# One attention-and-MLP kernel: reads put ahead of feature maps, first loads cut in pieces, and the weights' low bits moved to another engine

## The chip, the cores and the metric

The kernel runs on one core of one Trainium2 chip. The metric is the device time of one execution in microseconds, as the median of several runs; smaller is better. The engines are TensorE (PE, matmuls; PEld its weight loads), VectorE (DVE), ScalarE (ACT), GpSimd (POOL) and SyncE (SP), whose queue issues most DMAs.

## The reference

```python
scores = scale * q @ k.T                       # 4 batches, 8 heads, 576 tokens, 64 wide, causal
a = exp(scores - max); a /= a.sum() + 1e-9
local = a @ v
q_p = phi(q)                                   # where(x > 0, x, exp(x) - 1) + 1
mem_out = (q_p @ M_prev) / (q_p @ z_prev + 1e-6)
g = 1 / (1 + exp(-beta))
x = (g * mem_out + (1 - g) * local)            # reshaped to 2304 tokens x 512
out = (silu(x @ w_gate) * (x @ w_val)) @ w_out # 1536 hidden columns
```

q, k, v and the memory are float32; the three weight matrices are float64.

## The kernel before

Every fp32 operand of a large matmul is split into a high and a low part, and a product is three matmuls (high with high, high with low, low with high). The program has two stages.

**Attention.** The 32 head matrices are taken as 16 pairs. The loop at L532 runs 17 periods: period n does the scores and the softmax of pair n (`cur`) and, for pair n - 1 (`old`), the turning of the probabilities by transposes on TensorE (`turned`, `turned1`), the recall from the memory (`recall`), the products with v (`recalled`, `values`) and the result (`leave`, then `ending` in the next period, which casts the high part on ScalarE, subtracts the low part on VectorE and writes both to DRAM). Scores of one pair come in five steps t into the four banks `s`; VectorE reads a bank, adds the mask and finds the row's maximum (`reading`, the instruction CUSTOM_DVE_ANT_0), ScalarE takes the exponential (`exp`), VectorE inverts the sums (`rs`), and GpSimd scales the probabilities with the inverse and the gate (`weighed`, tiles `ps`, `pl` and `p`). The transposes and the products use four banks `tr` in turn. The work of each engine is kept in program order by `queued` (L79), so the order of the calls in the loop is the order on that engine. SP's DMAs and a few instructions that are issued by the bare engine names, such as `ACT.copy` at L279, are placed by the scheduler.

The first period is written out apart: `pair_load` (L248) loads q and k of a pair whole, for pair 0 with k from ScalarE's queue; `pair_split` cuts pair 0 in two column pieces; `phi_parts` (L326) makes the feature map of q with two ScalarE steps and one VectorE step (`SCALAR_TENSOR_TENSOR ph`); `gates` (L141) makes g and 1 - g from beta in two VectorE parts, `one_less` (needed by the first `weighed`) and `memory` (needed by the recall). In the first period `memory_gates`, `phi0` and the map of pair 1 come behind the exponential of step 4 (L594 to L597).

**Experts.** The hidden columns are 12 units f of 128, and the 2304 tokens are three blocks of 768 (L30). The first three units of the first block (`PLAIN`) compute gate and value straight (`eight`, four products of 12 matmuls); all others use a scheme with seven half-size products (`seven`) whose operands are sums and differences of weight quarters (`operands`) and of token quarters (`sums`). Two banks take the products in turn, six collect the output. A product's bank is free again when ScalarE has copied it or VectorE has weighed it (`weigh`).

Each unit has three weight matrices (gate, value, output): 36 "thirds" of 128 x 512 float64 words, made into fp32 in the first block and kept in DRAM for the other two. A third goes through: `raw_load` (DMA from SP), `raw_top` (ScalarE brings the upper word to scale, tile `we`, two buffers), `third_clamp` (tile `we`), `third_move` (the three bits of the lower word, tile `wa` or `wr`), `third_word` (VectorE joins both, SP writes it out, ScalarE casts the high part where it is wanted at once) and `low_part` (VectorE). The clamp and the move of the first four thirds run on VectorE within the attention (`EARLY`, L31), all others on GpSimd within the units of the first block (`third`, L234, at the steps of `plan`). On GpSimd the move reads only the last byte of the lower word, as

```python
eng.tensor_scalar(wa[n], last_byte, 1.0 / 32, 31.0 / 64, op0=ALU.mult, op1=ALU.subtract)
```

`plan[k]` lists what is issued behind product k of a unit. The sums of the first block's tokens (`due`) and their high and low parts (`spreads`, for p6, p5, p3, p7) are dealt out by hand over the first units at L880 to L893.

Of the kernel before, what the change touches and what calls it, by code (L numbers as in the profile page):

```python
# [9 lines left out]
F32 = mybir.dt.float32  # L10
F32R = mybir.dt.float32r
I32 = mybir.dt.int32
U8 = mybir.dt.uint8
AF = mybir.ActivationFunctionType
# [7 lines left out]
NP = B * NPAIR  # L22
# [22 lines left out]
def attention_moe(ctx: ExitStack, tc: tile.TileContext, qt, kt_, v, m, beta, wg, wv, wo, out):  # L45
# [70 lines left out]
    DVE.memset(warm, 0.0)  # L116
    ACT.activation(warm, warm, AF.Exp)
    maskp = const.tile([128, 512], F32, name="maskp")
    POOL.memset(maskp, 0.0)
# [42 lines left out]
    held, wout, wr = {}, {}, {}  # L162
    thirds = [(0, 0), (0, 1), (0, 2), (1, 0)]
    work_of = [[(1, 1), (3, 0), (3, 1)]]
    work_of += [[(n, 2)] + [(n + 1 + (n >= PLAIN - 1), j) for j in range(2)] for n in range(1, NF - 2)]
# [17 lines left out]
    def raw_top(act, n):  # L183
        if n < len(thirds):
            tops[n] = rot(wp, "we", [128, 512], F32, 2)
            act.activation(tops[n], raws[n][:, :, 1].bitcast(F32), AF.Prelu, scale=2.0**-111, alpha=2.0**32)
# [13 lines left out]
    def third_move(eng, n):  # L200
        f, j = thirds[n]
        if f < PLAIN or j == 2:
            wa[n] = rot(wp, "wa", [128, 512], I32, 3)
        else:
            if j == 0:
                wr[f] = rot(wp, "wr", [128, 1024], F32, 2)
            wa[n] = wr[f][:, j * 512 : j * 512 + 512].bitcast(I32)
        if eng is dve:
            eng.tensor_scalar(wa[n], raws[n][:, :, 0], 29, None, op0=ALU.logical_shift_right)
        else:  # L210
            last_byte = raws[n].rearrange("p a b -> p (a b)").bitcast(U8).rearrange("p (a b) -> p a b", b=8)[:, :, 3]
            eng.tensor_scalar(wa[n], last_byte, 1.0 / 32, 31.0 / 64, op0=ALU.mult, op1=ALU.subtract)

# [30 lines left out]
    with tc.tile_pool(name="sb", bufs=1, reuse_waits="tile") as sb:  # L244
# [3 lines left out]
        def pair_load(n):  # L248
            b, pr = divmod(n, NPAIR)
            qr = rot(sb, "qr", [128, 768], F32, NR)  # L250
            kr = rot(sb, "kr", [128, 576], F32, NR)
            for dst, src in ((qr, qt), (kr, kt_)):
                queue = ACT if n == 0 and dst is kr else SP
                loads[n] = queue.dma_start(dst, src[b, pr])
            return qr, kr
# [276 lines left out]
        for n in range(NP + 1):  # L532
# [6 lines left out]
            if cur:  # L539
                cur.begin()  # L540
            if old:
                old.turns()
# [7 lines left out]
            reads[1](0)  # L550
            reads[1](1)
            if after and n:
                after.split()
# [5 lines left out]
            turned(2, 0, dve)  # L559
            turned(2, 1, dve)  # L560
            exp(1, 1)
            scale = old.recall() if old else nothing
# [31 lines left out]
            if n == 0:  # L594
                memory_gates()
                phi0()
                phi = after.phi_parts()  # L597
            if old:
                old.recalled()
                old.values()  # L600
            if cur:
                cur.weighed(((2, 0), (2, 1), (3, 0), (3, 1)))
            phi()
            if cur:
                cur.weighed(((4, 0),))
            ending = old.leave() if old else lambda: nothing
# [5 lines left out]
            for i, at in enumerate(EARLY):  # L612
                if n == at:
                    raw_top(act, i)
                if n == at + 1:
                    third_clamp(dve, i)
                if n == at + (2 if i < 3 else 1):
                    third_move(dve, i)
                if n == at + (3 if i < 3 else 2):
                    third_word(act, dve, i)  # L620
                if n == at + (4 if i < 3 else 2):
                    low_part(dve)
            if n in AHEAD:
                raw_load(AHEAD.index(n), loads.get(n + 2))

        n = len(EARLY)
        raw_load(n + 3)
        raw_top(act, n)
        raw_top(act, n + 1)
        third_clamp(pool, n)  # L630
        third_move(pool, n)
        ending()()

    nj = N2 // 128
    with tc.tile_pool(name="stg2", bufs=1, reuse_waits="tile") as stg2, \
# [220 lines left out]
        for n, unit in enumerate(units):  # L856
# [14 lines left out]
            if n < len(units) - 1 and n + 1 >= PLAIN:  # L871
                ready[n + 1], work = operands(units[n + 1][1])
                if plain:
                    work = [work[0] + work[1], work[2], work[3], work[4] + work[5] + work[6]]
                for k, some_ in enumerate(work):
                    plan[k] += some_
# [3 lines left out]
            if plain:  # L880
                if f == 0:
                    _, due, mix = sums(t0, True)
                if f < 2:
                    for k in range(4):
                        plan[k].append(due[4 * f + k])
                if f == 1:
                    plan[2] += spreads(mix, ("h", "p6"))
                    plan[3] += spreads(mix, ("l", "p6"))
                if f == PLAIN - 1:
                    for k, p in ((0, "p5"), (1, "p3")):  # L890
                        plan[k] += spreads(mix, ("h", p))
                        plan[k + 2] += spreads(mix, ("l", p))
                    arrive = [(0, spreads(mix, ("h", "p7"))), (1, spreads(mix, ("l", "p7")))]  # L893
# [91 lines left out]
```

## Time and profile before

| | us |
|---|---|
| median of 3 runs | 626.1 (625.47 to 626.37) |
| the profiled execution | 626.68 |
| its span | 624.9 |
| TensorE busy in it | 604.7 |
| attention, to the first expert matmul | 193.9 |
| first token block, with the weights' conversion | 193.9 to about 345 |

All helper instructions carry one line (L84), so groups are told apart by tile names: `pl<-pl,rs,og` is a scaling, `s<-kh,qh` a matmul of scores, `wr<-wraw` a move of low bits. In a timeline a row has the start, the duration, the engine, the tiles, the shape and, in brackets, the idle time of that engine before it and the releaser. A busy TensorE is not TensorE at its best: its clock is in a column of its own.

### The profile page before, as it was taken

To read this page: it belongs to the slowest core of one execution; us is meant where nothing else is said; L and a number is where in the kernel's file an instruction comes from. 1 tells how busy PE (TensorE), PEld (TensorE's weight loads), DVE (VectorE), ACT (ScalarE), POOL (GpSimd) and SP (SyncE) were. 2 spreads that over 40 slices of the span, in tenths; PEclk is the share of its full clock that TensorE was granted. 3 is DMA by queue.
4 is the path that set the end of the run, shared out by engine and by line. 5 is a ranking of instruction groups with operands and counts; after the bars stand their busy time and mean duration, and the time that the engine had idled before them with its cause. 6 is when DMAs were issued, how large, how long until landed. Compare 5 with 4: busy or idle time off the path is not lost.

```text
span 624.9 us, 11274 instructions
## 1 busy us (share of the span) xinstructions
PE 604.7 (97%) x3794; PEld 534.9 (86%) x3794; DVE 494.7 (79%) x1209; ACT 383.5 (61%) x892; POOL 268.1 (43%) x282
## 2 busy tenths in 40 slices
PE   5999999999999899999999999999999999999997
PEld 3777788778778798988889999999999999999995
DVE  6799899999986899999999666566788765665653
ACT  6788888888875467666657644455446654454442
POOL 6899999999965986867740000000000000000000
PEclk9799999999999999999999999999999999999999
DMA  8355856757435775799638532232756631332212
GB/s 244 96 157 172 268 163 188 239 161 212 150 100 172 217 238 183 237 294 314 218 135 286 168 117 88 72 128 71 238 172 214 202 102 67 102 102 67 70 33 101
DMA packets 48745, 102.46 MB, mean 164 GB/s; under 512 B 6960, under 2 KB 16176, under 8 KB 48688
## 3 DMA queue, kind: packets, MB, share of 16 engines
q1 hardware_dynamic: 48544, 101.45, 50.1%
q8 instruction: 30, 0.49, 0.3%
q10 hardware_dynamic: 144, 0.29, 0.1%
q14 instruction: 27, 0.22, 0.1%
HBM read 74.99 MB, written 26.74 MB: 163 GB/s over the span
## 4 chain that ended last, share of the span: by engine, by line
PE 80%; DVE 9%; POOL 4%; ACT 3%; issue 2%; DMA 1%; DVEq 0%; POOLq 0%
PE s L84 50%; PE tr L84 30%; ACT pl L84 2%; DVE xr L84 1%; POOL we L84 1%; POOL wa L84 1%; DVE tl L84 1%; POOL wr L84 1%; DVE rs L84 1%; DVE pl L84 1%; DVE mem L84 1%; DMA kr<-in_kt_dram 1%; DVE zh L84 1%; ACT g L84 1%; DVE wa L84 1%
## 5 line engine op out<-in xcount | busy, mean ns | idle before, releaser
L84 POOL TENSOR_SCALAR pl<-pl,rs,og 128x384 f32<-128x384 f32 (+1 forms) x64 | 56.0, 886 | 10.9 <-DVE rs L84 10.9
L84 ACT ACTIVATE zh<-zh 128x384 f32<-128x384 f32 x33 | 17.3, 526 | 70.4 <-DVE zh L84 70.3
L84 PE MATMUL tr<-woh,uh 128*128 128x512 f32 x144 | 57.3, 398 | 0.0
L84 PE MATMUL tr<-wol,uh 128*128 128x512 f32 x144 | 56.7, 394 | 0.0
L84 PE MATMUL tr<-woh,ul 128*128 128x512 f32 x144 | 56.6, 393 | 0.0
L84 DVE TENSOR_TENSOR zv<-s,zv 128x384 f32<-128x384 f32 x33 | 18.3, 556 | 47.7 <-PE s L84 47.5
L84 ACT CAST th<-tt 128x512 fp32r<-128x512 f32 x66 | 41.0, 622 | 18.2 <-DVE tt L84 14.9
L84 ACT ACTIVATE pl<-pl,mx 128x384 f32<-128x384 f32 (+1 forms) x64 | 42.3, 663 | 14.2 <-DVE mx L84 14.2
L84 PE MATMUL tr<-g,vp 128*64 128x320 f32 (+4 forms) x448 | 48.7, 360 | 0.0
L84 DVE TENSOR_TENSOR tl<-tt,th 128x512 fp32r<-128x512 f32 x66 | 46.9, 711 | 0.0
L84 PE MATMUL s<-kh,qh 64*128 64x128 f32 (+4 forms) x160 | 37.6, 389 | 7.4 <-ACT kh L84 5.4
L84 PEld LDWEIGHTS tr<-g,vp 128*64 128x64 f32 x448 | 29.5, 137 | 17.6 <-issue 2.3
L84 POOL TENSOR_SCALAR we<-we 128x512 f32<-128x512 f32 x32 | 30.1, 940 | 28.1 <-ACT we L84 25.8
L84 POOL TENSOR_SCALAR wr<-wraw 128x512 int32<-128x512 uint8 x18 | 38.5, 2136 | 1.4
L84 DVE TENSOR_TENSOR zg<-s,zp 128x384 f32<-128x384 f32 x33 | 18.4, 558 | 25.9 <-ACT bh L84 20.6
L84 DVE CUSTOM_DVE_ANT_0 pl<-s,maskp 128x384 f32<-128x384 f32 (+1 forms) x64 | 38.1, 615 | 0.7 <-PE s L84 0.7
L84 ACT CAST uh<-zh 128x384 fp32r<-128x384 f32 x36 | 18.5, 514 | 29.7 <-DVE zh L84 29.4
L84 DVE TENSOR_TENSOR bl<-wr,bh 128x512 fp32r<-128x512 f32 x66 | 36.5, 553 | 0.0
L84 PE MATMUL tr<-ident,pl 128*128 128x128 f32 x224 | 32.3, 281 | 2.3 <-DVE xl L84 1.6
L84 POOL TENSOR_SCALAR ps<-ps,rs,og 128x128 f32<-128x128 f32 (+1 forms) x64 | 31.9, 511 | 6.0 <-DVE rs L84 5.1
L84 ACT CAST bh<-wr 128x512 fp32r<-128x512 f32 x66 | 33.9, 513 | 0.0
L84 DVE COPY g<-tr 128x384 f32<-128x384 f32 (+1 forms) x64 | 32.0, 519 | 2.1 <-PE tr L84 0.8
(187 smaller groups left out, 2031.6 us busy)
## 6 DMA issues: line engine op xcount, KB each, us to landing
wr<-wdr SPq DMA_DIRECT2D x24, 512.0 KB, 3.3
qr<-in_qt_dram SPq DMA_DIRECT2D x16, 384.0 KB, 3.1
wraw<-in_wg_dram SPq DMA_DIRECT2D x12, 512.0 KB, 4.4
wraw<-in_wv_dram SPq DMA_DIRECT2D x12, 512.0 KB, 4.8
wraw<-in_wo_dram SPq DMA_DIRECT2D x12, 512.0 KB, 4.4
wol<-wdo SPq DMA_DIRECT2D x24, 256.0 KB, 2.8
woh<-wdo SPq DMA_DIRECT2D x24, 256.0 KB, 3.2
vp<-in_v_dram SPq DMA_DIRECT2D x16, 320.0 KB, 4.4
```

The lines of the kernel that those rows point to most:

```text
L84: ins = getattr(eng, name)(*args, **kw)
```

## The change

Six things are edited.

1. Pair 0's q and k are loaded in five column pieces, three from SP and two from ScalarE's queue, those wanted first ahead.
2. The last scaling of pair 0, its feature map and the memory's gates (`late`) are issued in period 1 behind that period's first four reads; the VectorE step of pair 1's map goes to the end of period 1.
3. `third_move` for gate and value thirds runs on ScalarE (an Identity activation with scale and bias) where it ran on GpSimd; a bias tile is set at the start.
4. Third (1, 1) joins the early ones: in the last period its top, clamp, move and word are done, and so are the word of third (1, 0), which was already there, and the top of the next. The raw loads of thirds 7 and 8 follow. `we` has three buffers.
5. Silu's table is loaded at the start of the last period by an activation of one column.
6. In the plain units the sums, the spreads of p5 and the operands of unit 3 are dealt out over other steps.

```diff
+    low_bias = const.tile([128, 1], F32, name="low_bias")
+    DVE.memset(low_bias, -31.0 / 64)
...
-    thirds = [(0, 0), (0, 1), (0, 2), (1, 0)]
-    work_of = [[(1, 1), (3, 0), (3, 1)]]
+    thirds = [(0, 0), (0, 1), (0, 2), (1, 0), (1, 1)]
+    work_of = [[(3, 0), (3, 1)]]
...
-            tops[n] = rot(wp, "we", [128, 512], F32, 2)
+            tops[n] = rot(wp, "we", [128, 512], F32, 3)
...
             eng.tensor_scalar(wa[n], raws[n][:, :, 0], 29, None, op0=ALU.logical_shift_right)
+            return
+        last_byte = raws[n].rearrange("p a b -> p (a b)").bitcast(U8).rearrange("p (a b) -> p a b", b=8)[:, :, 3]
+        if j == 2:
+            eng.tensor_scalar(wa[n], last_byte, 1.0 / 32, 31.0 / 64, op0=ALU.mult, op1=ALU.subtract)
         else:
...
+            act.activation(wa[n], last_byte, AF.Identity, scale=1.0 / 32, bias=low_bias)
...
-            for dst, src in ((qr, qt), (kr, kt_)):
-                queue = ACT if n == 0 and dst is kr else SP
-                loads[n] = queue.dma_start(dst, src[b, pr])
+            if n == 0:
+                for queue, dst, src, c in (
+                    (SP, qr, qt, slice(128, 384)), (ACT, kr, kt_, slice(0, 256)), (SP, qr, qt, slice(384, 768)),
+                    (ACT, kr, kt_, slice(256, 576)), (SP, qr, qt, slice(0, 128)),
+                ):
+                    queue.dma_start(dst[:, c], src[b, pr, :, c])
+            else:
+                for dst, src in ((qr, qt), (kr, kt_)):
+                    loads[n] = SP.dma_start(dst, src[b, pr])
...
+            if n == NP:
+                act.activation(warm, warm, AF.Silu)
             if old:
                 old.turns()
...
             reads[1](1)
+            if n == 1:
+                for work in late:
+                    work()
             if after and n:
                 after.split()
...
             turned(2, 1, dve)
+            if n == NP:
+                for i in range(2):
+                    raw_top(act, len(EARLY) + i)
+                third_clamp(pool, len(EARLY))
+                third_move(pool, len(EARLY))
...
             if n == 0:
-                memory_gates()
-                phi0()
-                phi = after.phi_parts()
+                phi1 = after.phi_parts()
+            if n == NP:
+                for i in range(2):
+                    third_word(act, dve, len(EARLY) - 1 + i)
+                    raw_load(len(EARLY) + 3 + i)
...
-            phi()
-            if cur:
-                cur.weighed(((4, 0),))
+            if n == 0:
+                late = [lambda cur=cur: cur.weighed(((4, 0),)), phi0, memory_gates]
+            else:
+                if n == 1:
+                    phi1()
+                phi()
+                if cur:
+                    cur.weighed(((4, 0),))
...
-                if n == at + (3 if i < 3 else 2):
+                if n == at + 3 and i < 3:
                     third_word(act, dve, i)
-                if n == at + (4 if i < 3 else 2):
+                if n == at + 4 and i < 3:
                     low_part(dve)
...
-        n = len(EARLY)
-        raw_load(n + 3)
-        raw_top(act, n)
-        raw_top(act, n + 1)
-        third_clamp(pool, n)
-        third_move(pool, n)
         ending()()
+        low_part(dve)
+        i = len(EARLY) + 1
+        third_clamp(pool, i)
+        third_move(pool, i)
+        raw_top(act, i + 1)
...
-                    work = [work[0] + work[1], work[2], work[3], work[4] + work[5] + work[6]]
+                    work = [work[0] + work[1], work[2] + work[3], work[4] + work[5], work[6]]
...
-                if f < 2:
-                    for k in range(4):
-                        plan[k].append(due[4 * f + k])
+                    for k, some_ in enumerate(((0,), (1,), (2, 4), (3,))):
+                        plan[k] += [due[i] for i in some_]
                 if f == 1:
-                    plan[2] += spreads(mix, ("h", "p6"))
-                    plan[3] += spreads(mix, ("l", "p6"))
+                    for k in range(3):
+                        plan[k].append(due[5 + k])
+                    for k, p in ((0, "p5"), (2, "p6")):
+                        plan[k] += spreads(mix, ("h", p))
+                        plan[k + 1] += spreads(mix, ("l", p))
                 if f == PLAIN - 1:
-                    for k, p in ((0, "p5"), (1, "p3")):
-                        plan[k] += spreads(mix, ("h", p))
-                        plan[k + 2] += spreads(mix, ("l", p))
+                    plan[0] += spreads(mix, ("h", "p3"))
+                    plan[2] += spreads(mix, ("l", "p3"))
```

## Rows read from the trace of the kernel before

**Rows 1.** The page, part 1: busy us, share of the span, instructions.

```profile
PE 604.7 (97%) x3794; PEld 534.9 (86%) x3794; DVE 494.7 (79%) x1209; ACT 383.5 (61%) x892; POOL 268.1 (43%) x282
```

**Rows 2.** Timeline of PE, the first two periods, rows after idle time.

```profile
5.38 0.47 PE L84 MATMUL s<-kh,qh 64*128 64x128 f32 x2 [5.38 <-ACT kh L84]
...
13.82 0.38 PE L84 MATMUL s<-kh,qh 64*128 64x256 f32 x2 [1.39 <-DVE mx L84]
...
15.59 0.69 PE L84 MATMUL tr<-ident,ps 128*128 128x128 f32 x2 [0.56 <-POOL ps L84]
...
17.50 0.90 PE L84 MATMUL tr<-ident,pl 128*128 128x128 f32 x3 [0.30 <-POOL pl L84]
```

**Rows 3.** Windows: length, busy us by engine, granted clock, DMA share, GB/s.

```profile
15.50:22.00 6.50, 6.09 (x26) 4.75 (x28) 4.31 (x19) 4.40 (x13) 5.72 (x9) 0.50 0.19 61
22.00:24.00 2.00, 2.00 (x19) 1.59 (x16) 1.48 (x7) 1.07 (x3) 2.00 (x5) 0.99 0.06 12
```

**Rows 4.** Timeline of PE, the first token block, rows after idle time.

```profile
202.97 0.45 PE L84 MATMUL s<-xp1h,wgh 128*128 128x384 f32 x1 [0.47 <-ACT zh L84]
...
207.47 0.44 PE L84 MATMUL s<-xp1h,wgh 128*128 128x384 f32 x1 [2.11 <-DVE zh L84]
...
236.34 0.44 PE L84 MATMUL s<-xp7l,th 128*128 128x384 f32 x1 [0.56 <-DVE xp7l L84]
```

**Rows 5.** Waits of PE, whole span: us in total, times, longest.

```profile
PE s L84 <- DVE zg L84: 1.5, 4, 0.4
```

**Rows 6.** Timelines of ACT and POOL at the start: casts that wait for loads.

```profile
4.83 0.76 ACT L84 CAST kh<-kr 128x256 fp32r<-128x256 f32 x2 [2.18 <-DMA kr<-in_kt_dram]
...
8.37 0.67 ACT L279 CAST kh<-kr 128x576 fp32r<-128x576 f32 x1 [1.51 <-DMA kr<-in_kt_dram]
...
7.58 0.84 POOL L84 TENSOR_SCALAR qh<-qr 128x640 fp32r<-128x640 f32 x1 [1.89 <-DMA qr<-in_qt_dram]
```

**Rows 7.** The page, part 6: a DMA of 256 KB, median us to landing.

```profile
wol<-wdo SPq DMA_DIRECT2D x24, 256.0 KB, 2.8
```

**Rows 8.** Timelines of DVE and POOL, 14 to 17.5 us: feature maps and scalings.

```profile
14.30 0.81 DVE L84 SCALAR_TENSOR_TENSOR ph<-qe,ph 128x640 f32<-128x640 f32 x1
...
15.96 0.95 DVE L84 SCALAR_TENSOR_TENSOR ph<-qe,ph 128x640 f32<-128x640 f32 x1 [0.56 <-ACT ph L84]
...
14.33 1.21 POOL L84 TENSOR_SCALAR ps<-ps,rs,og 128x256 f32<-128x256 f32 x1
...
16.22 1.22 POOL L84 TENSOR_SCALAR pl<-pl,rs,og 128x384 f32<-128x384 f32 x1
```

**Rows 9.** Groups of POOL by shape, 184.1 to 187.3 us: busy, mean ns.

```profile
L84 POOL TENSOR_SCALAR pl<-pl,rs,og 128x384 f32<-128x384 f32 x2 | 1.3, 661 | 3.5 <-DVE rs L84 3.5
```

**Rows 10.** Timelines of ACT, DVE and PE in the last period and behind it.

```profile
195.41 1.28 ACT L84 ACT_TABLE_LOAD   x1
...
185.10 0.43 ACT L84 CAST xh<-tr 128x320 fp32r<-128x320 f32 x1 [0.45 <-PE tr L84]
...
185.99 0.48 DVE L84 TENSOR_TENSOR xl<-tr,xh 128x320 fp32r<-128x320 f32 x1
...
186.62 0.52 PE L84 MATMUL tr<-ident,pl 128*128 128x128 f32 x3 [0.43 <-POOL pl L84]
```

**Rows 11.** Groups of POOL, and of ACT from 190 us: busy, mean ns, idle before.

```profile
L84 POOL TENSOR_SCALAR wr<-wraw 128x512 int32<-128x512 uint8 x18 | 38.5, 2136 | 1.4
...
L84 ACT ACTIVATE we<-wraw 128x512 f32<-128x512 f32 x32 | 21.4, 672 | 8.8 <-DVE wr L84 8.6
```

**Rows 12.** Windows, one unit of the first block; busy PE, PEld, DVE, ACT, POOL.

```profile
255.00:266.50 11.50, 11.50 (x61) 10.70 (x61) 10.26 (x19) 7.31 (x16) 9.21 (x7) 1.00 0.70 229
```

**Rows 13.** Timeline of DVE ahead of the wait at 207.47.

```profile
204.97 0.69 DVE L84 SCALAR_TENSOR_TENSOR wr<-we,wr 128x512 int32<-128x512 int32 x1 [0.94 <-POOL wr L84]
205.58 1.36 DVE L84 TENSOR_TENSOR xr<-xp1h,xp1l 128x768 f32<-128x768 f32 x1
```

**Rows 14.** Groups of DVE by shape, 400 to 600 us (POOL at rest): mean ns.

```profile
L84 DVE TENSOR_TENSOR xr<-xr,xm 128x768 f32<-128x768 f32 x3 | 2.8, 949 | 0.0
```

More of the change, by code (lines that the diff above doesn't have):

```diff
@@ L209, in third_move @@
             eng.tensor_scalar(wa[n], raws[n][:, :, 0], 29, None, op0=ALU.logical_shift_right)
-        else:
-            last_byte = raws[n].rearrange("p a b -> p (a b)").bitcast(U8).rearrange("p (a b) -> p a b", b=8)[:, :, 3]
-            eng.tensor_scalar(wa[n], last_byte, 1.0 / 32, 31.0 / 64, op0=ALU.mult, op1=ALU.subtract)
+            return
+        last_byte = raws[n].rearrange("p a b -> p (a b)").bitcast(U8).rearrange("p (a b) -> p a b", b=8)[:, :, 3]
+        if j == 2:
+            eng.tensor_scalar(wa[n], last_byte, 1.0 / 32, 31.0 / 64, op0=ALU.mult, op1=ALU.subtract)
+        else:
+            act.activation(wa[n], last_byte, AF.Identity, scale=1.0 / 32, bias=low_bias)
     def third_word(act, dve, n):
```

## The prediction

> **What bounds the kernel now.** I read the page's first part, then TensorE's own timeline for its idle stretches, then what ended each, then the stages around them. TensorE is busy for 604.7 of 624.9 us [rows 1], so the kernel can gain only what TensorE loses: idle time and time at the lower clock. The idle 20.2 us have places. Before the first matmul lie 5.38 us. In the second period there are 1.39, 0.56 and 0.30 us; the reader is to see that the releasers are VectorE's reads and GpSimd's scalings [rows 2]. The granted clock there is 0.50 from 15.5 to 22 us, that is 1.2 GHz, after the idle time between 12.4 and 17.5 us, and back at 2.4 GHz after 22 us, behind a stretch without idle time [rows 3]. The first token block loses 0.47, 2.11 and 0.56 us at three places [rows 4] and 1.5 us in four waits for the product that VectorE weighs [rows 5]: 4.68 us in all (0.47 + 2.11 + 0.56 + 1.54). The tail behind the last matmul (about 4.6 us) and the rest of the attention are not touched. So some 12 us of idle time (5.38 + 2.25 + 4.68) are within the reach of this change, and the time at half clock besides.
>
> **The sum.** It is made against the profiled execution (626.68 us, its span 624.9); the median of the runs shown is 626.1, 0.58 lower, and I take the sum off the median.
>
> **1. First loads in pieces.** TensorE starts at 5.38 because ScalarE's first cast waits for the load of k, which with q is 672 KB and lands at 4.8 [rows 2, 6]. In pieces, the first two are 256 KB together. The nearest row is a 256 KB load that lands 2.8 us after its issue [rows 7] against 4.1 here (0.71 to 4.8), so the first matmul comes up to 1.3 us earlier. What gives that back is the second pair. Two more DMA issues stand ahead of its q and k on SP's queue, some 0.4 us each, and today those land just in time: ScalarE waits 1.51 us for k, until 8.37, GpSimd 1.89 us for q, until 7.58 [rows 6]. ScalarE's exponentials of the first pair and then the gates' are queued behind that cast, and GpSimd's split of the second pair ends at 11.44, only 1.5 us before the first scaling at 12.92. One more issue ahead of the table load on ScalarE ends long before data is there. So between -1.3 (all of it) and +0.8 (nothing gained, the second pair late by two issues); I take -0.5, since the second pair's landing is the nearer limit.
>
> **2. Second period's reads ahead of gates and feature maps.** VectorE's two feature-map instructions (0.81 and 0.95 us) today lie at 14.30 and 15.96, and GpSimd's scalings that run beside them take 1.21 and 1.22 us [rows 8] where a scaling of 384 columns takes 0.66 with nothing beside it [rows 9] and one of 256 no more. That is 1.1 us too much (0.55 twice), and TensorE's transposes at 15.59 and 17.50 wait for exactly these scalings [rows 2]. With VectorE at PSUM reads instead, the chain to 17.50 shortens by up to 1.1. The maps come after the four reads, before 17 us; the first is needed at 18.3 by the recall, and the last scaled pair of rows is a GpSimd step queued later but still ahead of its transposes at 24.5. ScalarE's second-period exponentials come about 1.5 us earlier, which no matmul waits for. The 1.39 us at 13.82 stay: that read already stood ahead of the maps. From 17.5 to 22 us TensorE has work without a pause at half clock; if the rise stays where it is, work done earlier there is worth half. I take -0.8 of 1.1, bounds 0 and -1.1, and keep the clock as a rival: 6.09 busy us at half clock [rows 3] are worth at most 3.0.
>
> **3. Silu's table early.** Its load (1.28 us) leaves 195.41, where no matmul waits for it, and goes with its 0.2 us activation right after ScalarE's cast that ends at 184.65, ahead of the one that starts at 185.10 [rows 10]. That cast slips to about 186.15, VectorE's low part behind it from 185.99 to 186.6, and TensorE's transpose at 186.62, which takes the bank that this low part has just read (it ends at 186.47), slips with it [rows 10]: +0.6. Here a rule speaks against the change. The Trainium skill, "ScalarE: Activation LUTs", section "What ACT_TABLE_LOAD costs", gives a load 1283 ns and a drain of about 1380 ns besides; by it this would be about +2.0 and the whole sum 1.4 worse. The trace agrees with the load and shows no drain (the cast before it had just ended, and Silu starts 0.01 us behind it), so the sum goes by the trace. Bounds 0 and +1.0 (another order of the casts; the three further ScalarE steps that the last period now gets, 2.0 us, fit into its 2.3 us wait ahead of the next copy, with little to spare). VectorE's two word instructions moved ahead of the recall fall into its 1.7 us of idle time there.
>
> **4. Low bits on ScalarE.** GpSimd's shift from the last byte costs 2.14 us each [rows 11] and runs on the 32 thirds that are not done early; 21 of them (gate and value) move to ScalarE, and the 11 of the output weights stay. ScalarE's nearest form, the same 512 elements at the same 8-byte stride, takes 0.67 [rows 11] (672 ns); the other bound is GpSimd's 2.14 for the same bytes. I take 0.67: both are single-input elementwise passes of ScalarE. In a unit of 11.5 us ScalarE is busy 7.31, VectorE 10.26, GpSimd 9.21 [rows 12]: two moves make ScalarE 8.65 and GpSimd 4.9. The move stands ahead of one bank copy, which today ends 1.6 us before its bank is wanted; 0.67 fits. Its raw word is on chip, since the top of the same third was read two steps earlier. The third "we" buffer takes away ScalarE's wait for VectorE's word.
>
> What it gives: the 2.11 us at 207.47 come from VectorE's weighing, which stood behind a word that waited 0.94 us for GpSimd's shift and behind a sum of 1.36 us [rows 13], and such a sum takes 0.95 with GpSimd at rest [rows 14]. Gone with the shift, and with one third fewer in the first unit (its word, 0.69, and the low part after it, 0.68, now done while TensorE runs the recall): 0.69 + 0.94 + 2 x 0.41 = 2.4 us earlier, so 2.11 and the 0.47 before it go. Late next is VectorE in the second unit: I count 13.1 us of instructions against 12.5 us of matmuls, behind which it recovers in the third, where I count 10 against 12.5. The 0.56 us (the low part of p7, late because p5 and p3 crowd the third unit) go, since p5 moves to the second unit and the operands of the fourth unit start a step earlier. Of the 1.54 us in four waits, 1.0 go: VectorE is 10.26 of 11.5 busy, and loses less to GpSimd, but the shift of the output weights that still runs beside the late sum stays. Together -4.1, bounds -4.7 (all) and -1.5 (half of the 2.58, little else). The raw loads of thirds 7 and 8 stand 5 us later on SP's queue than the one load today (186.1), behind the words at 191; at a landing of 4.4 us they are there at 195.5, two us before ScalarE takes their top.
>
> Sum: -0.5 - 0.8 + 0.6 - 4.1 = -4.8, so 626.1 - 4.8 = **621.3 us**.
>
> **The rivals.**
> The clock comes back earlier in the second period, or never falls, since less idle time lies between 12 and 17.5 us: 2 us of the 3.0 more, 619.3. For it: the idle time ahead of the fall shrinks by 1.1. Against: the 1.39 us that start it stay. 12%.
> VectorE stays the bound in the first token block, and waits change their names: step 4 gives -1.5 instead of -4.1, 623.9. For it: 13.1 against 12.5 us in the second unit. Against: the third unit's slack. 15%.
> The change does not do what it says: the second pair's loads, late by two issues, cost the start 0.8, the table load its bound of 1.0, and step 4 gives its lower end of 1.5 with part 2 at zero: +0.3, about 626.4, no change. 10%.
> Slower: ScalarE's move of the low bits is dear. It uses a function (Identity) that the trace of before does not show. If that is not in the table that holds Silu, each move brings two loads of 1.28 [rows 10], 3.24 us in all; 7.31 + 6.5 is 13.8 in a unit of 11.5, in seven units +16 us: 641. It decides from 2.1 us per move on, (11.5 - 7.31) / 2; GpSimd's price of 2.14 [rows 11] for the same bytes would sit right there. Against it: casts and the tops run beside Silu without a load. 8%. The Trainium skill, "ScalarE: Activation LUTs", section "Table sets: the hidden batching unit", says that identity is in every set; no run here shows it.
>
> **How the numbers follow.** The forecast has 55%. The three faster cases add to 82% (55 + 12 + 15); within 0.2% (1.25 us, about what a measurement of this kernel can tell from no change) 10%; slower 8%. The range reaches from the clock's case with most of step 4's remainder (-4.8 - 2.0 - 0.6 and 0.5 of the start, 618.2) to the case of VectorE and another 0.9 of the start (624.8).
>
> **What would show it.** The first matmul near 4.1 to 4.8 us instead of 5.38; scalings beside 15 us at 0.7 instead of 1.2; the transpose at 17.50 near 16.2; the clock's half-speed stretch; the table load near 184.7 and the transpose after it about 0.6 later; ScalarE's move at 0.67; no wait over 0.5 us between 195 and 240; VectorE's sums near 1.0. The forecast is wrong if waits of TensorE in the first token block still sum to over 2 us, if the table load delays by over 1 us, or if a second table load shows up beside the moves.

## The result, and the profile after

The changed kernel takes 619.18 us in the median (618.62 to 620.03), beside 625.79 us for the kernel before: a ratio of 0.990 (95% interval 0.988 to 0.992), 6.6 us less. The forecast was 621.3 us, 4.8 us less. The profiled execution took 619.71 us, its span is 617.9 us.

The page's first part (the answer to [rows 1]):

```profile
PE 602.4 (97%) x3794; PEld 535.6 (87%) x3794; DVE 486.1 (79%) x1210; ACT 394.5 (64%) x914; POOL 217.1 (35%) x261
```

GpSimd lost 51.0 us of work and ScalarE gained 11.0. TensorE's idle time went from 20.2 to 15.5 us (617.9 - 602.4). TensorE's timeline, rows behind idle time in the first two periods, with the first recall between them (to [rows 2]):

```profile
4.24 0.47 PE L84 MATMUL s<-kh,qh 64*128 64x128 f32 x2 [4.24 <-ACT kh L84]
...
11.49 0.33 PE L84 MATMUL s<-kl,qh 64*128 64x128 f32 x2 [0.53 <-POOL kl L84]
...
13.62 0.58 PE L84 MATMUL s<-kh,qh 64*128 64x256 f32 x2 [1.69 <-DVE mx L84]
...
17.12 1.28 PE L84 MATMUL tr<-mm,ph 128*128 128x130 f32 x10
...
21.69 0.40 PE L84 MATMUL s<-kh,qh 128*128 128x288 f32 x1 [0.83 <-DVE mx L84]
```

The first matmul is 1.14 us earlier, but the scores at 13.62 only 0.20: the second pair's split by GpSimd (`kl`) is late now. The idle time at 15.59 and 17.50 is gone. There is a new wait of 0.83 us at 21.69. Windows with the granted clock behind POOL's busy time (to [rows 3]):

```profile
13.50:17.00 3.50, 3.38 (x18) 3.15 (x19) 3.00 (x17) 3.40 (x9) 3.50 (x6) 0.52 0.54 182
17.00:19.00 2.00, 2.00 (x20) 1.88 (x20) 1.47 (x6) 2.00 (x8) 2.00 (x4) 0.99 0.48 172
```

TensorE is granted 2.4 GHz again from 17 us on, where it was 22 us. That is not the edits' doing alone: in e9 and e10 (below), whose first two periods are the same code, it is granted 2.4 GHz again only from 20.9 and 18.9 us on. In the expert stage no wait of TensorE is left ([rows 4, 5] have no counterpart). The unit of [rows 12] reads now:

```profile
255.00:266.50 11.50, 11.50 (x61) 10.75 (x60) 9.77 (x19) 8.63 (x18) 4.34 (x4) 1.00 0.88 266
```

VectorE 9.77 us instead of 10.26, ScalarE 8.63 (forecast 8.65), GpSimd 4.34 (forecast 4.9).

To place the gain I follow the same matmuls through every trace and subtract their start times. Columns: first matmul; first recall; third recall; third to fifteenth recall; fifteenth recall to the first expert matmul; from there to the 667th matmul behind it (the first token block but for its end; the weights are converted in it); from there to the last matmul; then the median of all runs and the ratio to the kernel before. All in us, of one profiled execution each.

| kernel | 1st | rec 1 | rec 3 | 3 to 15 | to experts | block | rest | median | ratio (95%) |
|---|---|---|---|---|---|---|---|---|---|
| before | 5.38 | 18.31 | 42.00 | 134.49 | 17.42 | 134.30 | 291.70 | 625.8 | 1 |
| after | 4.24 | 17.12 | 40.20 | 134.10 | 17.97 | 128.40 | 292.35 | 619.2 | 0.990 (0.988 to 0.992) |
| e1 | 5.40 | 17.02 | 40.54 | 133.93 | 17.97 | 128.49 | 292.35 | 620.4 | 0.991 (0.990 to 0.993) |
| e2 | 4.18 | 17.21 | 40.57 | 133.46 | 17.95 | 128.45 | 292.35 | 620.9 | 0.992 (0.991 to 0.994) |
| e3 | 4.25 | 16.82 | 39.76 | 133.61 | 17.43 | 128.42 | 292.35 | 619.0 | 0.989 (0.987 to 0.990) |
| e4 | 4.20 | 16.35 | 39.53 | 133.53 | 17.97 | 128.91 | 292.35 | 620.1 | 0.991 (0.989 to 0.992) |
| e5 | 5.52 | 18.45 | 41.92 | 134.01 | 17.44 | 130.25 | 292.35 | 622.8 | 0.995 (0.994 to 0.997) |
| e6 | 5.26 | 18.16 | 41.91 | 133.96 | 17.42 | 135.40 | 291.70 | 628.0 | 1.003 (1.001 to 1.004) |
| e7 | 5.22 | 18.16 | 41.31 | 133.94 | 17.43 | 128.77 | 292.35 | 621.0 | 0.993 (0.991 to 0.995) |
| e8 | 5.41 | 19.27 | 44.05 | 133.39 | 17.42 | 133.33 | 292.02 | 625.7 | 1.000 (0.998 to 1.001) |
| e9 | 4.16 | 18.59 | 41.78 | 134.64 | 17.42 | 128.46 | 292.35 | 619.4 | 0.989 (0.987 to 0.991) |
| e10 | 4.13 | 17.63 | 40.65 | 133.00 | 18.02 | 128.41 | 292.33 | 619.3 | 0.989 (0.988 to 0.991) |
| e11 | 4.26 | 16.25 | 40.30 | 134.66 | 17.95 | 128.76 | 293.01 | 620.0 | 0.990 (0.988 to 0.991) |
| e12 | 4.18 | 16.91 | 40.52 | 134.14 | 18.02 | 128.75 | 293.03 | 621.1 | 0.991 (0.989 to 0.992) |

Before to after, at the last matmul: -1.80 up to the third recall, -0.39 in the periods after it, +0.55 in the last period, -5.90 in the block, +0.65 in the rest: -6.89 us. The column "3 to 15" scatters from 133.0 to 134.7 over all kernels, so its -0.39 is not read.

The first columns scatter too, among kernels whose code is the same there: the third recall comes at 39.53 to 41.78 us in after, e3, e4, e9 and e10, and at 41.31 to 44.05 in before, e5, e6, e7 and e8. In the first five nearly all of it goes back to one load, in the other five a part. GpSimd's cast of the second pair's q starts when that q has landed, at 6.99 to 9.12 us in the first five. Counted from that cast, the first recall comes 9.35 to 9.64 us later in these five and 10.44 to 11.23 us later in the other five, and the third recall 32.48 to 32.66 and 33.59 to 36.02 us later. So the gain up to the third recall (1.80 us, or 34.42 - 32.49 = 1.93 from the landing) is clear of the scatter, and a single trace's differences are read from the landing below.

### The profile page after: what moved, and what is told of

Its sections match the earlier page's. It is cut to its first block, busy times and chain, and to the rows that moved or that the text cites. A ratio compares the mean times of both kernels' runs of the same rounds, so it can differ in the third digit from the quotient of the medians.

```text
span 617.9 us, 11275 instructions
## 1 busy us (share of the span) xinstructions
PE 602.4 (97%) x3794; PEld 535.6 (87%) x3794; DVE 486.1 (79%) x1210; ACT 394.5 (64%) x914; POOL 217.1 (35%) x261
## 4 chain that ended last, share of the span: by engine, by line
PE 91%; DVE 5%; ACT 2%; issue 1%; DMA 1%; DVEq 0%; ACTq 0%
PE s L84 58%; PE tr L84 33%; ACT pl L84 1%; DVE rs L84 1%; DVE mem L84 1%; DVE pl L84 1%; DVE xl L84 1%; DMA kr<-in_kt_dram 0%; ACT g L84 0%; DVE w L84 0%; DVE ph L84 0%; DMA out_dram<-pt 0%; DVE wa L84 0%; ACT xh L84 0%; DVE gs L84 0%
## 5 line engine op out<-in xcount | busy, mean ns | idle before, releaser
L84 ACT ACTIVATE zh<-zh 128x384 f32<-128x384 f32 x33 | 17.4, 528 | 75.9 <-DVE zh L84 75.9
L84 POOL TENSOR_SCALAR we<-we 128x512 f32<-128x512 f32 x32 | 27.7, 867 | 76.0 <-ACT we L84 75.8
L84 PEld LDWEIGHTS tr<-woh,ul 128*128 128x128 f32 x144 | 27.0, 188 | 7.1 <-DVE ul L84 0.3
L84 PEld LDWEIGHTS tr<-ident,pl 128*128 128x128 f32 x224 | 25.3, 143 | 9.0 <-POOL pl L84 3.5
```

Source lines behind the costliest of these rows:

```text
L84: ins = getattr(eng, name)(*args, **kw)
```

## The experiments

### The first token block: which part brings the 5.9 us

**e4, the move of the low bits back on GpSimd** (all else as after):

```diff
-            act.activation(wa[n], last_byte, AF.Identity, scale=1.0 / 32, bias=low_bias)
+            eng.tensor_scalar(wa[n], last_byte, 1.0 / 32, 31.0 / 64, op0=ALU.mult, op1=ALU.subtract)
```

> The changed kernel with the low bits of gate and value thirds back on GpSimd; the early fifth third, the other order of the sums and the third buffer stay. Theory A: ScalarE's move is what clears the waits of the first token block, and they come back: 3.5 to 6 us slower than the changed kernel (5.9 were gained in that block). Theory B: the early third and the new order clear the waits at 203 to 236 us, and the move only the four small ones: 1 to 2.5 us slower.

The block takes 128.91 instead of 128.40 us, with no wait of TensorE in it. VectorE and GpSimd are nearly as busy as in [rows 12]:

```profile
255.00:266.50 11.50, 11.50 (x62) 10.70 (x61) 10.42 (x19) 7.51 (x15) 8.86 (x7) 1.00 0.86 277
```

So in the block of the changed kernel the move is worth 0.5 us, though it takes 4.5 us of GpSimd's work out of this unit (8.86 - 4.34). The waits were gone without it.

**e5, the move alone, put into the kernel before.**

```diff
-            eng.tensor_scalar(wa[n], last_byte, 1.0 / 32, 31.0 / 64, op0=ALU.mult, op1=ALU.subtract)
+            if j == 2:
+                eng.tensor_scalar(wa[n], last_byte, 1.0 / 32, 31.0 / 64, op0=ALU.mult, op1=ALU.subtract)
+            else:
+                act.activation(wa[n], last_byte, AF.Identity, scale=1.0 / 32, bias=low_bias)
```

> The kernel before (625.8 us) with the move of gate and value thirds on ScalarE and nothing else. From the first expert matmul to the last it takes 426.0 us before and 420.8 after the change; with the low bits back on GpSimd it took 421.3. Theory A: the move clears the waits by itself too (it and the rest are two ways to the same gain): 422 us or less in that stage, 3.5 to 4.5 us faster in all. Theory B: the rest does it and the move is worth 0.5 us wherever it stands: about 425.5, and 0.5 us faster.

The block is 4.05 us shorter, 130.25. TensorE's waits from 192 to 335 us (us in total, times, longest) are what is left of [rows 4, 5]:

```profile
PE s L84 <- DVE zg L84: 1.0, 4, 0.3
PE s L84 <- DVE zh L84: 0.2, 1, 0.2
```

**e6, the new dealing-out alone** (the edits of `plan`, `due` and `spreads` in the kernel before):

```diff
-                    work = [work[0] + work[1], work[2], work[3], work[4] + work[5] + work[6]]
+                    work = [work[0] + work[1], work[2] + work[3], work[4] + work[5], work[6]]
...
-                if f < 2:
-                    for k in range(4):
-                        plan[k].append(due[4 * f + k])
+                    for k, some_ in enumerate(((0,), (1,), (2, 4), (3,))):
+                        plan[k] += [due[i] for i in some_]
```

> The kernel before with only the sums, the spreads of p5 and the operands of the fourth unit dealt out anew. Theory A: it clears the wait for p7's low part (0.56 us and the restart behind it) and none of the others: 0.7 to 1.0 us less in the expert stage (about 425.1). Theory B: it loads VectorE more in the first two units, where GpSimd is the bound, and gives nothing or costs up to 1 us.

The block is 1.10 us longer. The same view of its waits:

```profile
PE s L84 <- DVE zh L84: 4.1, 2, 3.4
PE s L84 <- DVE zg L84: 1.5, 4, 0.4
PE s L84 <- ACT zh L84: 0.4, 1, 0.4
```

The 0.56 us for `xp7l` are gone, as the prediction's step 4 has it, but a wait of 0.61 us for `zh` at 233.15 has come in their place, and the wait of 2.11 us has grown to 3.44: more work stands ahead of the weighing. Put in alone, this part makes the kernel slower.

**e7, the early third with the third buffer, alone** (part 4 of the change, nothing else, in the kernel before; the moves in the units stay on GpSimd):

```diff
-    thirds = [(0, 0), (0, 1), (0, 2), (1, 0)]
-    work_of = [[(1, 1), (3, 0), (3, 1)]]
+    thirds = [(0, 0), (0, 1), (0, 2), (1, 0), (1, 1)]
+    work_of = [[(3, 0), (3, 1)]]
...
-            tops[n] = rot(wp, "we", [128, 512], F32, 2)
+            tops[n] = rot(wp, "we", [128, 512], F32, 3)
```

> The kernel before with the fifth third done in the last period and the third buffer for the tops; no other edit. Theory A: one of GpSimd's chains of 3.8 us less in the first unit clears the waits at 203 and 207 us (2.6 us idle and two restarts), and with the third buffer the four small ones: 4 us or more less in the expert stage (422 or less). Theory B: the first two waits only shrink, by a third: about 424.5.

The block takes 128.77 us, 5.53 less, and has no wait of TensorE at all. This part alone brings nearly the whole gain of the block. Whether the changed kernel needs it, with the move on ScalarE as well, is not shown: no run undoes it there. e4 is e7 with the start, the table load and the dealing-out of the change; their blocks (128.91 and 128.77) say that the dealing-out adds nothing.

**e8, the third buffer alone.**

```diff
-            tops[n] = rot(wp, "we", [128, 512], F32, 2)
+            tops[n] = rot(wp, "we", [128, 512], F32, 3)
```

> The kernel before with a third buffer for the tops and nothing else. Theory A: ScalarE's tops no longer wait for VectorE's words (8.6 us of such waits before), GpSimd's chain runs ahead, and the four waits at 279 to 316 us go: 1.5 to 2 us less in the expert stage, about 424.2. Theory B: GpSimd is the bound of that chain and not the buffer: within 0.4 us of before.

0.97 us in the block, none in the median. One wait is left, and it is longer than the 2.11 us of before:

```profile
PE s L84 <- DVE zh L84: 2.8, 1, 2.8
```

The 0.97 us are too low a price for the buffer. Behind that wait the granted clock falls in this execution, as it does in no other trace's expert stage:

```profile
209.75:213.00 3.25, 3.25 (x11) 2.87 (x10) 2.98 (x4) 1.72 (x3) 3.17 (x2) 0.50 0.67 225
```

3.4 us at 1.2 GHz with TensorE busy throughout cost up to 1.7 us by my estimate. The runs say the same: the three of e8 with a mean granted clock of 0.994 take 623.2 to 624.0 us, the twelve of the kernel before with 0.993 or more take 624.6 to 626.7. So the buffer seems worth about 2 us where the clock stays up. It takes the small waits away (0.1 us and less is left of each), and the early third, put in beside it in e7, the large one; the early third without the buffer was not run. The move alone (4.05) and the early third with its buffer (5.53) are two ways to the same gain; together they give 5.9, not 9.6.

### The first two periods

**e1, pair 0 loaded whole** (all else as after):

```diff
-                for queue, dst, src, c in (
-                    (SP, qr, qt, slice(128, 384)), (ACT, kr, kt_, slice(0, 256)), (SP, qr, qt, slice(384, 768)),
-                    (ACT, kr, kt_, slice(256, 576)), (SP, qr, qt, slice(0, 128)),
-                ):
-                    queue.dma_start(dst[:, c], src[b, pr, :, c])
...
+            for dst, src in ((qr, qt), (kr, kt_)):
+                queue = ACT if n == 0 and dst is kr else SP
+                loads[n] = queue.dma_start(dst, src[b, pr])
```

> The changed kernel (619.2 us) with q and k of pair 0 loaded whole again. Theory A: the pieces bring the first matmul 1.14 us forward (5.38 to 4.24), but the second pair binds behind it: GpSimd's split of it ends at 11.44 us in both kernels, VectorE's gate sum is held until then, and the scalings start only 0.27 us earlier. Then whole loads put the first matmul back to about 5.4, the scalings to about 12.9, and cost 0.2 to 0.5 us in all. Theory B: the 1.14 us are carried through to the recall, and whole loads cost 1.0 to 1.3 us (or more, if the clock then rises later).

TensorE's timeline, the two rows behind idle time that answer to 4.24 and 13.62:

```profile
5.40 0.48 PE L84 MATMUL s<-kh,qh 64*128 64x128 f32 x2 [5.40 <-ACT kh L84]
...
13.84 0.39 PE L84 MATMUL s<-kh,qh 64*128 64x256 f32 x2 [1.08 <-DVE mx L84]
```

The start is 1.16 us later and at 13.84 all but 0.22 of it has vanished; the third recall is 0.34 later. The median is 1.2 us higher with intervals that overlap, so the runs place the pieces' worth between 0.3 and 1.2 us, between the two theories. What binds is the landing of the second pair's q: from GpSimd's cast of it to the first recall e1 takes 9.41 us, as the five traces with pieces do (9.35 to 9.64), and to the third 32.92 (32.48 to 32.66). That cast starts at 7.54 to 8.04 us in the six kernels with whole loads (7.70 in the mean), and at 6.83 to 9.12 us in the eight with pieces (7.59). So the pieces bring the landing no clear gain, and scatter it.

**e2, gates and feature maps back in the first period** (`late` dissolved: `memory_gates`, `phi0` and the map of pair 1 are issued where the kernel before has them):

```diff
-            if n == 1:
-                for work in late:
-                    work()
...
+                memory_gates()
+                phi0()
```

> The changed kernel with the feature maps, the memory's gates and the last scaling of pair 0 back in the first period, ahead of the second period's reads. Theory A: they hold up GpSimd's scalings (1.2 us each instead of 0.55 to 0.66), TensorE idles for them again, the stretch at half clock grows from 3.4 us to 6.8, and the kernel is 1.5 to 2.5 us slower, all of it before 26 us. Theory B: the clock's earlier rise came from the first loads; then the scalings alone cost, 0.5 to 1.0 us.

GpSimd's first four scalings, here and in the kernel after (start and duration), which took 2.61 us in the kernel before:

```profile
11.81 2.63 POOL L84 TENSOR_SCALAR ps<-ps,rs,og 128x128 f32<-128x128 f32 x4 [1.22 <-DVE rs L84]
```

```profile
12.65 1.98 POOL L84 TENSOR_SCALAR ps<-ps,rs,og 128x128 f32<-128x128 f32 x4 [1.22 <-DVE rs L84]
```

In e2 the second pair landed 0.88 us earlier than in after (6.83 against 7.71), so I count from that landing: the third recall lies 33.74 us behind it in e2, 32.49 in after. That makes 1.25 us (the five traces with the code of after lie at 32.48 to 32.66), and the first recall, 10.38 us behind the landing, is back near the 10.44 to 11.23 of the kernels with the code of before; the median says 1.7. The size that the first theory gave (1.5 to 2.5) fits the median and not quite the trace.

**e11, the gate's sum on ScalarE.** In after, VectorE's smallest instruction here is held, as its row and GpSimd's show:

```profile
10.40 1.06 DVE L84 TENSOR_SCALAR gs<-gs 128x8 f32<-128x8 f32 x1
...
10.03 1.41 POOL L84 TENSOR_TENSOR kl<-kr,kh 128x576 fp32r<-128x576 f32 x1
```

Eight columns take 1.06 us, until GpSimd's subtraction ends (10.03 + 1.41 = 11.44). In the kernel before, the same sum starts when that subtraction is over and takes 0.17 us. The Trainium skill, "SBUF — State Buffer", section "SBUF: two separate sides", says that VectorE and GpSimd share a pair of ports, and that a GpSimd instruction, or a VectorE instruction in a two-port mode or with two inputs from SBUF, holds it for its whole length. The row fits that, for an instruction this small too; no row shows which mode the sum runs in. The edit:

```diff
+        act.activation(gs, gs, AF.Identity, bias=one)
...
-            dve.tensor_scalar(gs, gs, 1.0, None, op0=ALU.add)
```

(with a tile `one`; in period 1 the first scalings and their sums, `first`, are placed behind the recall's scaling, `scale`).

> The changed kernel with two of VectorE's sums with a constant taken out of GpSimd's way: the gate's 1 + exp on ScalarE (one more step of 0.2 us there), and in the second period the sums of the first scalings behind the recall's scaling. Theory A: GpSimd's elementwise instructions hold these sums until they end (1.06 us instead of 0.17, twice: until GpSimd's split ends at 11.44 and its next at 20.15); without them the second-period scores at 13.62 come 0.3 to 0.9 us earlier, the wait of 0.83 us at 21.69 shrinks to under 0.3, and the kernel is 0.7 to 1.5 us faster. Theory B: something else holds VectorE there (an operand), and the next instruction takes over the wait: within 0.3 us of the changed kernel.

VectorE's reciprocal, which came behind that sum, now starts at 10.41 instead of 11.50, and it is not held, though GpSimd's subtraction still runs:

```profile
10.41 0.20 DVE L84 RECIPROCAL gs<-gs 128x8 f32<-128x8 f32 x1
...
9.20 1.42 POOL L84 TENSOR_TENSOR kl<-kr,kh 128x576 fp32r<-128x576 f32 x1
```

The first recall comes at 16.25, 0.87 us earlier, but that is the load: the second pair landed 0.85 us earlier than in after (6.86 against 7.71), and from the landing the first recall takes 9.39 us (after 9.41). To the third it takes 33.44, longer than the 32.48 to 32.66 of after's code. So the first theory's gain is not there, in the trace or in the median. The expert stage became 1.0 us longer (128.76 - 128.40 and 293.01 - 292.35), which the last section takes up.

**e12, e11 with the edits of e9 and e10** (below).

> The changed kernel with the three edits of the runs before together. If each does what its theory A says, they lie in different stretches and add: 0.5 + 2.1 + 1.1 = 3.7 us faster than the changed kernel, about 615.5 us. If only the late words and the table do, 616.6.

No gain: 0.991 (0.989 to 0.992). It has a use of its own, since TensorE's clock does not fall before the last matmul in this execution. Windows from the first to the second recall of e12, of after and of e11; the granted clock is the third number from the end:

```profile
16.91:29.44 12.53, 12.15 (x103) 9.51 (x102) 11.00 (x39) 8.76 (x26) 10.99 (x15) 1.00 0.35 99
```

```profile
17.12:29.12 12.00, 11.17 (x104) 8.87 (x102) 11.11 (x39) 8.62 (x26) 11.05 (x15) 1.00 0.35 96
```

```profile
16.25:29.23 12.98, 12.93 (x103) 10.57 (x103) 10.48 (x39) 8.65 (x24) 10.92 (x15) 0.83 0.33 92
```

With the whole stretch at 2.4 GHz (1.00) this way takes 12.5 and 12.0 us, with part of it at 1.2 GHz 13.0 (and 12.47 in the kernel before). VectorE and GpSimd are busy 11 us of it. So the full clock shortens the period by 1 us at most, and in e12 by nothing against before.

The runs of one code say more. After, e3 and e4 have the full clock from 16.2 to 17.4 us on and need 11.86 to 12.10 us for this way; e10 and e9, with the half clock until 18.9 and 20.9 us, need 11.94 and 12.11. With 2.4 GHz from 17 us on, TensorE meets the wait of 0.83 us at 21.69; in e9, at 1.2 GHz until 20.9, it meets none up to the third recall:

```profile
17.00:19.00 2.00, 2.00 (x11) 2.00 (x10) 1.97 (x5) 2.00 (x9) 2.00 (x3) 0.50 0.34 81
```

In the changed kernel, then, TensorE does not set the pace here. That VectorE and GpSimd do fits their busy time; no run shows it by itself. In the kernel before the clock does count: e8, the same code there, has the half clock until 25.4 us where before, e5 and e6 have it until 22, and it needs 24.78 us from the first recall to the third where they need 23.47 to 23.75.

### The last period

**e3, no early load of Silu's table** (all else as after):

```diff
-            if n == NP:
-                act.activation(warm, warm, AF.Silu)
```

> The changed kernel without the early load of Silu's table, so that it stands ahead of the first Silu again. Theory A: the early load costs TensorE 0.55 us (its wait in the last period is 0.98 instead of 0.43 us) and gives nothing, since ScalarE idles 0.64 us ahead of the first Silu and the bank is wanted 1.8 us later: 0.5 us faster than the changed kernel, about 618.7. Theory B: the load at its use makes the first Silu late, and a wait in the first unit takes back 0.5 us or more: no gain, or slower.

The last period takes 17.43 us instead of 17.97, and the expert stage is unchanged: where the table is first used, no matmul waits for it. Timelines of after (ScalarE, VectorE, TensorE) around the load, and of e3's transpose:

```profile
182.12 0.35 ACT L84 CAST xh<-tr 128x256 fp32r<-128x256 f32 x1
182.49 1.28 ACT L84 ACT_TABLE_LOAD   x1
183.79 0.20 ACT L84 ACTIVATE warm<-warm 128x1 f32<-128x1 f32 x1
183.90 0.41 ACT L84 CAST xh<-tr 128x320 fp32r<-128x320 f32 x1
...
184.33 0.49 DVE L84 TENSOR_TENSOR xl<-tr,xh 128x320 fp32r<-128x320 f32 x1 [0.45 <-ACT xh L84]
...
184.97 0.52 PE L84 MATMUL tr<-ident,pl 128*128 128x128 f32 x3 [0.98 <-DVE xl L84]
```

```profile
183.50 0.52 PE L84 MATMUL tr<-ident,pl 128*128 128x128 f32 x3 [0.44 <-DVE xl L84]
```

This is the chain of the prediction's step 3: load, cast, low part, transpose; TensorE's wait is 0.98 instead of 0.44 us. e3 has the lowest median of all (619.0), but its interval overlaps with that of after.

**e9, the table loaded at the end of the last period, behind the loop.**

```diff
-            if n == NP:
-                act.activation(warm, warm, AF.Silu)
...
+        act.activation(warm, warm, AF.Silu)
```

> The changed kernel (619.2 us) with Silu's table loaded at the end of the last period, behind the words and the cast of the first result columns, where ScalarE idles 1.32 us, and not at its start. Theory A: the early load's whole price is the 0.55 us by which TensorE's transpose slips, and 1.32 us of idle time hide 1.48 us of load and activation but for 0.16, which no matmul waits for: the last period is back at 17.4 us (18.0 in the changed kernel), 0.5 us faster. Theory B: the first unit needs ScalarE then, and a wait shows there.

17.42 us, as e3, and an unchanged block. The median (0.989) doesn't show the half microsecond. The profiled execution is a poor one: the second pair landed at 9.12 us, and the third recall is 1.6 us later than in after.

**e10, the first three words and their low parts each a period later** (`third_word` at the head of period `at + 4`, `low_part` in `at + 5`).

```diff
-                if n == at + 3 and i < 3:
-                    third_word(act, dve, i)
-                if n == at + 4 and i < 3:
+                if n == at + 5 and i < 3:
```

> The changed kernel with the words of the first three early thirds one period later, behind the exponential of step 4, and their low parts one period later too. Theory A: TensorE's three waits for VectorE's low part (0.54, 0.59 and 0.57 us idle at 74, 118 and 163 us, a restart of about 0.25 us behind each) come from the word and the cast that stand ahead of it; they go, and the kernel is 1.7 to 2.5 us faster. Theory B: the late place takes VectorE's time in that period and a wait for another of its steps takes their place: within 0.5 us.

The three waits of 0.54 to 0.59 us for `xl` at 74.0, 118.5 and 162.9 shrink to two of 0.24 us and three for VectorE's reads, 0.5 us together (after has two, 0.4). The twelve periods take 133.00 us, the least of all kernels, 1.1 less than in after and about half of what the first theory wanted. But e12, which has the same edit, takes 134.14, and the median shows nothing, so the gain is not shown.

## Why the prediction was right or wrong

**Step 1, pieces.** Right. The first matmul came at 4.24 (forecast 4.1 to 4.8), and the second pair's landing gave most of it back: -0.20 at 13.62, -0.34 at the third recall by e1, against a forecast of -0.5. That the landing moves by over 2 us between traces with pieces was not foreseen.

**Step 2, reads ahead.** Right in mechanism: the scalings take 0.50 us each (1.98 / 4) and the transposes at 15.6 and 17.5 no longer wait. The gain was 0.63 us in four scalings, and the recall is 1.19 us earlier. Of the 1.1 us (0.55 twice) only the first half vanished. The `pl` scalings take as long as before, first in the kernel before, then in after:

```profile
15.57 3.37 POOL L84 TENSOR_SCALAR pl<-pl,rs,og 128x384 f32<-128x384 f32 x4
```

```profile
14.62 3.39 POOL L84 TENSOR_SCALAR pl<-pl,rs,og 128x384 f32<-128x384 f32 x4
```

The feature map, now at 15.62, runs beside the third of them, where it ran beside the second, and for the third no transpose waits. Steps 1 and 2 together were to give 1.3 us; the third recall shows 1.80.

**The clock's rival** happened in part: the half-clock stretch ends at 17 instead of 22 us in the profiled execution, and at 18.9 and 20.9 in e10 and e9. Its price was wrong for the changed kernel. I valued busy time at half clock at full worth, as if TensorE set the pace there. That is nearer the truth in the kernel before (e8: 1.1 us for 3.4 us more at half clock, 1.7 at full worth), but with the reads ahead it does not hold: e10 and e9 reach the third recall 32.48 and 32.66 us behind the landing, after, e3 and e4 32.49 to 32.58, and e12, without any half clock, 32.64.

**Step 3, Silu's table.** Right to a tenth: +0.6 forecast, +0.55 measured, +0.54 by e3. In the row of the load the cast before it ends at 182.47 and Silu's column starts 0.02 us after the load: no drain. By the drain that the Trainium skill gives ("ScalarE: Activation LUTs", section "What ACT_TABLE_LOAD costs") it would have been near +2.0; the measurement decides.

**Step 4, the low bits.** Here the prediction failed, in its size and in its cause. It gave -4.1; the block shows -5.9, more than its bound of -4.7. Three points:

- The size. The bound summed idle times, and a wait costs TensorE more than its idle bracket. In the kernel before, the matmul ahead of [rows 4]'s second wait starts at 205.02, the waiting one at 207.47 and the next at 207.74: 2.72 us for two matmuls that take 0.17 each elsewhere, 2.37 lost, for a bracket of 2.11. Read so against the same matmuls in after, the seven waits with 4.68 us of idle time cost 5.80, nearly all of the 5.9: the three of [rows 4] 0.26 to 0.34 us each above their brackets, the four of [rows 5] 0.06 or 0.07. The rest of the miss is that all 1.54 us of these four went, where step 4 took 1.0.
- The cause. "Gone with the shift, and with one third fewer in the first unit" added the two as terms of one sum (0.69 + 0.94 + 0.82 = 2.4 us). e5 and e7 show that either clears the waits of [rows 4], all but 0.15 us: 4.05 and 5.53 us. In the changed kernel the move is worth 0.5 (e4). For the four small waits the move was not the main cure either: alone it takes them from 1.54 to 1.03 us (e5), the third buffer alone to 0.1 and less each (e8).
- The dealing-out. "The 0.56 us go, since p5 moves": they go in e6, but they go as well in e5, e7 and e8 without it, and alone it brings a wait of 0.61 us in their place and makes the wait for the weighing 1.3 us longer.

The rival in which VectorE stays the bound did not come: 13.1 us of instructions in the second unit against 12.5 delayed no matmul, as no wait shows up. VectorE's sums came as foreseen: seven of the eight between 193 and 240 us take 0.94 or 0.95 us, where six of eight took 1.36 or 1.37.

**The slower rival** is out. ScalarE's moves, by shape, from 183 to 345 us, with all table loads:

```profile
L84 ACT ACTIVATE wr<-wraw,low_bias 128x512 int32<-128x512 uint8 x18 | 13.7, 764 | 0.0
...
L84 ACT ACTIVATE wa<-wraw,low_bias 128x512 int32<-128x512 uint8 x3 | 2.3, 760 | 0.0
...
L84 ACT ACT_TABLE_LOAD x1 | 1.3, 1283 | 0.0
```

21 moves of 0.76 us (forecast 0.67) and one table load: Identity runs beside Silu. The Trainium skill, "ScalarE: Activation LUTs", section "Table sets: the hidden batching unit", has identity in every set, and the trace agrees.

**Not foreseen:** +0.65 us in the rest, where nothing was edited. The misses partly cancel: -0.5 (start), -1.8 (block), +0.65; with the -0.39 that is not read they make the 2.1 us between -4.8 and -6.89.

## What to carry to other kernels

Where two edits feed the same wait, price each as if the other were done: their gains don't add. Put each in alone and undo each alone: e5 put in the move and it looked worth 4.05 us, e4 undid it and it was worth 0.5. A wait on TensorE costs more than its idle bracket, so take its price from the starts of the matmuls around it. An earlier start is worth only what the next load lets through. And before two traces are compared, look how far traces of the same code differ there, and from which event on they agree.

## What the runs showed of the hardware that was not expected

The pace of matmuls differs between these programs, beyond their instructions. The column "rest" holds the same matmuls at a granted clock of 1.00 without waits, yet it takes 291.70 us in the kernel before and in e6, 292.02 in e8 (a `we` buffer more), 292.33 to 292.35 in all kernels with the tile `low_bias` (one column of 4 bytes), and 293.01 and 293.03 in e11 and e12, which have a second such tile. It hardly differs among kernels with the same tiles, whatever else they do. By form, 400 to 600 us, the means shift by a few ns; after, then e11:

```profile
L84 PE MATMUL tr<-wol,uh 128*128 128x512 f32 x70 | 27.5, 392 | 0.0
...
L84 PE MATMUL s<-xp1h,bl 128*128 128x384 f32 x36 | 12.1, 337 | 0.0
```

```profile
L84 PE MATMUL tr<-wol,uh 128*128 128x512 f32 x69 | 27.3, 396 | 0.0
...
L84 PE MATMUL s<-xp1h,bl 128*128 128x384 f32 x36 | 12.2, 340 | 0.0
```

So the bias column goes with 0.65 us less gain, 0.2% of the pace, and the second one in e11 with as much again. It is not the chip: e5 to e8 ran on one and take 292.35, 291.70, 292.35 and 292.02. It is not the column's use: in e7 no instruction reads the tile, and it shows the same 292.35. I suspect where the operands' tiles come to lie in SBUF, since each added tile moves those behind it; no run moved a tile without adding one, so that is open.
